# A linear-attention and snake-MLP kernel on one core: all engine orders planned anew, zero matmuls in other places

## The chip, the core and the metric

The kernel runs on one core of one Trainium2 chip. Its engines are TensorE (PE, with its weight loads as PEld), VectorE (DVE), ScalarE (ACT), GpSimd (POOL) and SyncE (SP); SP issues nearly all DMAs. The metric is the device time in microseconds; lower is better.

## The reference

Two layers stand one behind the other. The first is a gated linear attention with a decaying state, the second an MLP whose activation is a snake function:

```python
f = 1.0 / (1.0 + np.exp(-f_logit))                      # batch 4, heads 8, seq 768, head_dim 48
for t in range(S):
    state = f[:, :, t, :, None] * state + np.einsum('bhd,bhe->bhde', k[:, :, t], v[:, :, t])
    y[:, :, t] = np.einsum('bhd,bhde->bhe', q[:, :, t], state)
x = y.transpose(0, 2, 1, 3).reshape(B * S, H * D)       # 3072 tokens x 384
h = x @ w_in                                            # 384 -> 2048
s = np.sin(alpha * h)
out = (h + s * s / (alpha + 1e-09)) @ w_out             # 2048 -> 384
```

## The kernel before, in words

**Work.** The sequence is cut in chunks of 128 tokens, and the attention is done by chunks. The inputs come in 12 units `u` = 0 to 11. A unit has four loads of 384 KB, named here by letter and unit: f5 is the gate logits of unit 5, q5 its queries, k5 its keys, v5 its values. Units 0 to 3 cover two chunks of one batch each, in runs of 384 bytes; units 4 to 11 cover one chunk of two batches each, in runs of 192 bytes (`load`, L247 to L259). A unit holds two pairs, numbered `m` = 2u and 2u + 1. So q5 serves pairs 10 and 11.

**Steps of a unit** (`pre`, L332): ACT takes exp and ln of the gate (L341, L350), PE sums the logs (`cs_`, L359 and L365), ACT makes G and its inverse Gi (L373, L376), and POOL or DVE multiply the keys by Gi and the queries by G (`mul`, L383, tile qk). `values` (L353) casts v to bf16, mostly on POOL.

**Steps of a pair** (`attend_two` for units 0 to 3, `attend` from unit 4): PE transposes keys and queries (`transposed`, L414; called kt and qt with the pair's number here), DVE or ACT copy the result out, PE makes the scores (`a_`, L467 or L549), DVE masks them (L472 or L553), PE makes y from the state (`inter_`, L489 or L558) and from the chunk (`intra_`, L484 or L564) and the new outer products (`kv_`, L497 or L569), and DVE and POOL update the state (L575, L418). From pair 16 on the transposes of keys and queries are DMAs (L586).

**Steps of the MLP.** `x_of` copies y to bf16 (tile yn, L426) and transposes it, for groups 0 to 2 on PE (L430, copied out at L434), for groups 3 to 5 by a DMA from SP (tile xT, L444). A group is 512 tokens, with four y tiles numbered 0 to 3. `first` and `first_half` (L619, L638) make h in PSUM, ACT takes the sine (L604), DVE adds (L607, tile g). `second` (L656) multiplies g by w_out, ACT or DVE copy the result out (tile osb, L662), SP stores it (L666). The weights are loaded in eight pieces into a ring of three buffers (`w_in` L289, `w_out` L311) and folded to bf16 by DVE or ACT (L296, L317, L319).

**What sets the order.** The program first collects all operations (`op`), 956 of them, each with the engines that can run it and a planner's costs. It then issues them in the sequence of the list `ORDER` (`in_order`). An entry x is a packed number: the operation is x modulo 2000, the choice among its engines is x // 2000 % 5, the PSUM bank of the tile that it takes is x // 10000 % 10 (and x // 1000000 for a second tile), and x // 100000 % 10 is a number of zero matmuls that PE runs ahead of it. A zero matmul is 128 x 512 elements of a zeroed tile, written to the bank that the next operation takes (L704); it has no result that is used. The engines run their own queues in this order, each strictly from front to back, and wait for one another by semaphores. The buffers in SBUF come from rings (`SLOTS`), and a load waits until its buffer is free. The costs and the `dma=` figures in the source were the planner's inputs; `in_order` doesn't read them, so only `ORDER` reaches the chip.

Of the kernel before, what the change touches and what calls it, by code (L numbers as in the profile page):

```python
# [17 lines left out]

ORDER = [2, 78, 79, 720081, 82, 6, 140, 141, 400143, 40144, 60000, 4, 84, 3, 86, 90, 83, 10, 2085, 50091, 92,
    2088, 2089, 70095, 96, 5, 1, 202, 7, 145, 94, 2080, 2130105, 93, 14, 2097, 8, 2087, 63, 51, 98, 146, 40099,
    147, 102, 106, 240, 70153, 150, 2151, 130157, 2148, 100, 2149, 203, 4060101, 241, 103, 9, 107, 158, 50062,
    2160, 1030104, 109, 108, 154, 2110, 2152, 205, 159, 2155, 2113, 64, 30111, 65, 2112, 55, 206, 20050, 208,
    156, 207, 30114, 59, 40243, 60164, 2115, 2211, 20244, 100161, 130054, 53, 52, 246, 12, 165, 245, 2142, 162,
    20119, 7060167, 150116, 168, 2210, 120, 56, 117, 40163, 1050166, 57, 2172, 171, 60122, 2175, 121, 169, 170,
    40173, 16, 123, 118, 176, 2177, 2248, 2174, 10125, 2213, 30137, 20134, 40187, 124, 126, 66, 15, 11, 127, 69,
    50178, 58, 138, 139, 135, 188, 70184, 60181, 136, 2068, 179, 61, 10199, 247, 30193, 60, 189, 180, 2249, 212,
    131, 182, 2067, 20190, 40716, 50253, 254, 209, 250, 72, 185, 132, 717, 183, 60128, 2214, 186, 256, 75, 255,
    70215, 216, 13, 50726, 194, 195, 727, 133, 30196, 736, 71, 2070, 129, 737, 738, 739, 200, 201, 191, 18, 218,  # L30
    728, 10706, 729, 2217, 707, 130, 60219, 192, 2073, 2251, 220, 70257, 258, 718, 2074, 17, 77, 2252, 740, 197,
    222, 259, 221, 2260, 719, 720, 721, 2204, 198, 22, 310, 708, 709, 20, 60226, 76, 20223, 730, 311, 227, 741,
    722, 710, 349, 742, 224, 743, 2242, 744, 60313, 40314, 19, 723, 316, 20264, 23, 315, 731, 350, 724, 732,
    733, 24, 40229, 265, 2318, 2322, 2734, 7060225, 2321, 7030228, 2234, 20261, 711, 26, 230, 233, 2237, 231,
    40352, 40353, 735, 262, 317, 60235, 320, 712, 2070267, 232, 354, 21, 359, 236, 268, 30263, 6030266, 25, 355,
    2360, 713, 60323, 70238, 272, 271, 324, 269, 30, 30273, 2714, 2275, 10336, 239, 2274, 70375, 276, 2357, 28,
    325, 270, 376, 40326, 356, 337, 745, 2277, 20286, 420, 2358, 377, 60378, 33, 2338, 40287, 421, 288, 328,
    327, 379, 2312, 40302, 10362, 363, 303, 364, 329, 2361, 60294, 330, 304, 60295, 282, 296, 289, 305, 283,
    297, 20278, 284, 60279, 285, 40298, 280, 40299, 38, 37, 60290, 4351, 281, 20291, 306, 2528, 2319, 60307,
    300, 20766, 767, 292, 301, 30776, 768, 34, 27, 777, 40423, 60424, 778, 293, 308, 426, 309, 769, 60372, 373,  # L40
    70346, 770, 771, 425, 457, 772, 559, 365, 40339, 347, 773, 60333, 70380, 381, 779, 2429, 2428, 780, 340,
    725, 29, 374, 2774, 781, 526, 782, 31, 366, 20341, 458, 40746, 430, 342, 783, 747, 460, 432, 461, 49, 2784,
    382, 431, 343, 70367, 427, 334, 32, 368, 30331, 369, 20433, 527, 434, 748, 50445, 60344, 348, 446, 70385,
    749, 750, 435, 462, 467, 715, 2422, 463, 2447, 345, 335, 20370, 383, 2465, 332, 386, 2371, 2384, 751, 752,
    60436, 2468, 20448, 50450, 2387, 449, 753, 408, 20409, 560, 437, 2754, 20392, 410, 40442, 443, 40393, 394,
    775, 411, 60388, 36, 389, 390, 2466, 40482, 395, 483, 2651, 451, 2452, 396, 60397, 2469, 39, 20400, 401,
    2484, 398, 42, 50438, 439, 391, 60404, 440, 46, 60405, 43, 40412, 413, 453, 399, 785, 464, 402, 406, 444,
    414, 416, 60417, 403, 30796, 20756, 407, 797, 60562, 418, 415, 757, 758, 2459, 40563, 798, 40454, 40, 419,
    564, 799, 50470, 471, 529, 565, 20530, 800, 41, 759, 760, 455, 60485, 472, 40473, 570, 486, 761, 532, 569,
    762, 531, 801, 10786, 755, 2537, 816, 474, 35, 60479, 649, 650, 70487, 488, 763, 817, 764, 2489, 441, 536,  # L50
    802, 40475, 787, 44, 566, 535, 534, 70556, 20491, 818, 788, 582, 476, 549, 803, 492, 804, 4561, 789, 819,
    820, 490, 2477, 478, 790, 20583, 40550, 791, 792, 2571, 456, 624, 493, 625, 793, 821, 480, 2538, 45, 557,
    60585, 822, 584, 2794, 70552, 823, 551, 20589, 2568, 805, 48, 586, 553, 40494, 40495, 558, 533, 2554, 795,
    587, 496, 60518, 824, 506, 590, 60519, 520, 539, 497, 40507, 508, 20502, 20503, 40498, 20499, 521, 2567,
    2626, 60510, 509, 47, 504, 500, 60511, 806, 807, 808, 809, 501, 505, 810, 40652, 40653, 811, 812, 512, 813,
    513, 20627, 40628, 655, 10836, 837, 657, 572, 654, 2656, 838, 588, 60540, 40573, 2814, 839, 826, 827, 828,
    629, 481, 765, 829, 574, 40846, 541, 630, 20514, 515, 2633, 50575, 825, 632, 830, 2659, 576, 658, 555,
    60522, 516, 2634, 40523, 847, 848, 849, 850, 840, 577, 517, 50542, 841, 660, 591, 524, 831, 631, 842, 667,
    20661, 525, 662, 60668, 843, 543, 669, 2544, 851, 852, 832, 50546, 833, 642, 834, 578, 20856, 30579, 580,
    635, 581, 545, 853, 857, 670, 2844, 858, 859, 547, 671, 2854, 60636, 845, 40643, 30663, 637, 860, 2672, 644,  # L60
    861, 862, 548, 855, 863, 2864, 608, 40609, 610, 673, 835, 664, 2665, 60596, 20597, 598, 815, 666, 20645,
    611, 40592, 593, 30638, 639, 604, 594, 599, 646, 20605, 2647, 640, 595, 60600, 20601, 606, 641, 607, 20612,
    40866, 602, 613, 648, 620, 603, 867, 614, 621, 622, 615, 623, 865, 60616, 868, 50896, 897, 898, 899, 900,
    617, 869, 870, 20694, 20695, 901, 618, 876, 619, 696, 877, 878, 902, 903, 871, 60674, 697, 10886, 904, 872,
    879, 880, 20678, 873, 20675, 676, 874, 20679, 40686, 60687, 677, 881, 882, 887, 60690, 883, 888, 691, 680,
    688, 2884, 681, 689, 905, 692, 20682, 906, 683, 693, 907, 40698, 60699, 684, 875, 885, 685, 60702, 20703,
    20936, 937, 908, 938, 909, 939, 940, 910, 30916, 941, 704, 917, 705, 918, 60926, 927, 928, 929, 919, 889,
    700, 701, 942, 943, 911, 912, 913, 2914, 930, 931, 932, 933, 934, 944, 915, 920, 921, 890, 891, 922, 923,
    2924, 945, 925, 892, 893, 935, 70946, 947, 948, 949, 950, 951, 952, 894, 895, 953, 2954, 955]

SLOTS = dict(f=3, k=3, q=3, v=3, lf=2, qk=6, vb=4, gl=6, Gi=2, tr=4, at=3, xT=2, yn=4, s=3, g=18, G=2, osb=4, sum=2,
             wst=3, st0=2, st1=2, st2=2, st3=2)
# [15 lines left out]
def in_order(ops):  # L88
# [5 lines left out]
    held = {n: [(None, -1)] * k for n, k in SLOTS.items()}  # L94
    for nth, x in enumerate(ORDER):
        o = ops[x % 2000]
# [15 lines left out]
def kernel(  # L112
# [19 lines left out]
    B, H, S, D = q.shape  # L132
# [18 lines left out]
    PE, ACT, DVE, POOL, SP = "PE", "ACT", "DVE", "POOL", "SP"  # L151
# [10 lines left out]
    def op(engs, emit, deps=(), takes=(), holds=(), table=None, dma=None, after=0):  # L162
        o = Op(engs, emit, [d for d in deps if d is not None], list(takes), table, dma, after)
        o.uses = set(takes) | set(holds)
        for b in o.uses:
            b.users.append(o)
        ops.append(o)
        return o
# [10 lines left out]
    def at(b):  # L179
        return T[b.ring][b.place]  # L180
# [66 lines left out]
    def load(u, n):  # L247
        b = bufs[n, u] = Buf(n)

        def emit(e):  # L250
            if u < B:
                dst = at(b).rearrange("c (h j) d -> c h (j d)", j=2)
                src = srcs[n][u * H:(u + 1) * H, :2 * C, :].rearrange("h (c j) d -> c h (j d)", j=2)
            else:
                c, bp = divmod(u, NU)
                dst = at(b)
                src = srcs[n][bp * 2 * H:(bp + 1) * 2 * H, c * C:(c + 1) * C, :].rearrange("b c d -> c b d")
            engine[e].dma_start(out=dst, in_=src)  # L258
        b.ready = op({SP: 500}, emit, takes=[b], dma=1240 if u < B else 1800)  # L259

    bufs, made = {}, {}

# [409 lines left out]
    for u in range(NCH * NU):  # L672
        for n in "fkqv":
            load(u, n)
# [61 lines left out]
```

## Time and profile before

| | |
|---|---|
| median of 5 runs | 184.59 us (184.44 to 185.94) |
| span of the profiled execution | 184.5 us |
| device time of the profiled execution | 186.25 us |
| PE busy | 175.1 us, 95% |
| DVE, ACT, POOL busy | 138.3, 126.6, 65.3 us |
| DMA moved | 33.48 MB, 181 GB/s on average |

The profiled execution took 186.25 us, of which 184.5 lie between its first and its last instruction; it is 1.66 us above the median of the runs that were not profiled. Its rows are compared with its own span, and only differences are carried over to the median. PE is shown as busy while a matmul is anywhere in its pipeline, so the durations of single matmuls overlap; the time that one costs is read from start to start.

### The profile page before, as it was taken

What the parts mean: (1) busy time and instruction counts of PE and PEld (TensorE: products, weight loads), DVE (VectorE), ACT (ScalarE), POOL (GpSimd) and SP (SyncE); (2) the same over time, 40 slices, a digit from 0 to 9 for tenths busy, and PEclk for the clock granted to TensorE, in tenths of its full rate; (3) what the DMA queues carried; (4) which work ended last, traced back from release to release, by engine and by line L of the source; (5) the groups of instructions that cost most, each with busy time, mean ns of one, the idle gap of its engine ahead of it and who ended that gap; (6) DMA issues with size and microseconds to landing.
All of it is one profiled execution on the core that took longest, in us unless ns stands there. A gap on an engine that the chain in (4) does not pass through costs nothing.

```text
span 184.5 us, 4401 instructions
## 1 busy us (share of the span) xinstructions
PE 175.1 (95%) x1773; PEld 107.4 (58%) x1773; DVE 138.3 (75%) x185; ACT 126.6 (69%) x171; POOL 65.3 (35%) x107
## 2 busy tenths in 40 slices
PE   6698999899996999999999999999999999999993
PEld 2366678666673546675556764455675555555662
DVE  4679999898885898888697885799785874375511
ACT  2959997789786989899979557895336744164311
POOL 7396215661486202959304783047030000000000
DMA  5999999999999999999999869938733310111014
GB/s 156 322 335 358 320 310 273 317 331 198 192 156 240 197 249 219 213 239 230 224 205 193 182 137 261 179 96 101 151 110 107 62 45 4 43 45 40 0 68 149
DMA packets 103516, 33.48 MB, mean 181 GB/s; under 512 B 96684, under 2 KB 101948, under 8 KB 103496
## 3 DMA queue, kind: packets, MB, share of 16 engines
q1 hardware_dynamic: 103440, 33.17, 76.4%
q8 instruction: 14, 0.23, 0.5%
q14 instruction: 6, 0.05, 0.1%
q10 hardware_dynamic: 56, 0.03, 0.1%
HBM read 25.20 MB, written 4.72 MB: 162 GB/s over the span
## 4 chain that ended last, share of the span: by engine, by line
PE 71%; DMA 17%; SPq 4%; ACT 3%; POOL 1%; DVE 1%; issue 1%; POOLq 0%; ACTq 0%
PE banks L619 28%; PE banks L656 27%; DMA wst<-in_moe_w_out_dram 5%; DMA v<-in_v_dram 4%; DMA q<-in_q_dram 4%; PE banks L359 3%; SPq L258 3%; PE banks L414 3%; DMA xT<-yn 2%; PE banks L549 2%; DMA f<-in_f_logit_dram 2%; PE banks L564 2%; PE banks L558 1%; PE banks L365 1%; PE banks L704 1%; PE banks L569 1%
## 5 line engine op out<-in xcount | busy, mean ns | idle before, releaser
L656 PE MATMUL banks<-w_out_bf,g 128*128 128x384 bf16 (+1 forms) x400 | 72.3, 320 | 0.0
L607 DVE SCALAR_TENSOR_TENSOR g<-s,banks 128x1024 bf16<-128x1024 f32 (+1 forms) x56 | 57.4, 1064 | 15.3 <-ACT s L604 15.2
L604 ACT ACTIVATE s<-banks 128x1024 f32<-128x1024 f32 (+1 forms) x56 | 49.2, 902 | 20.0 <-PE banks L619 19.5
L619 PE MATMUL banks<-xT,w_in_bf 128*128 128x512 bf16 x240 | 56.4, 379 | 0.2 <-DMA xT<-yn 0.2
L656 PEld LDWEIGHTS <-g 128*128 128x128 bf16 x400 | 36.1, 98 | 21.1
L619 PEld LDWEIGHTS <-w_in_bf 128*128 128x128 bf16 x240 | 22.5, 98 | 23.9 <-issue 0.2
L383 POOL TENSOR_TENSOR qk<-q,G 128x384 bf16<-128x384 f32 x18 | 18.7, 1047 | 21.8 <-PE banks L359 8.4
L383 POOL TENSOR_TENSOR qk<-k,Gi 128x384 bf16<-128x384 f32 x20 | 20.4, 1032 | 17.0 <-DMA v<-in_v_dram 9.6
L553 DVE TENSOR_TENSOR at<-banks,mask 128x1024 bf16<-128x1024 f32 x16 | 18.8, 1218 | 4.2 <-PE banks L549 4.0
L662 ACT COPY osb<-banks 128x384 f32<-128x384 f32 (+1 forms) x14 | 6.6, 468 | 15.2 <-PE banks L656 15.2
L353 POOL CAST vb<-v 128x768 bf16<-128x768 f32 x10 | 9.1, 911 | 19.7 <-DMA v<-in_v_dram 19.7
L341 ACT ACTIVATE f<-f 128x768 f32<-128x768 f32 x12 | 10.0, 845 | 5.1 <-DMA f<-in_f_logit_dram 5.1
L414 PE MATMUL banks<-ident,qk 128*128 128x128 bf16 x128 | 10.7, 224 | 2.5 <-POOL qk L383 2.4
L662 DVE COPY osb<-banks 128x384 f32<-128x384 f32 (+1 forms) x11 | 5.8, 536 | 9.6 <-PE banks L656 9.6
L418 POOL TENSOR_TENSOR st<-sum,gl 128x384 bf16<-128x384 f32 x11 | 9.4, 858 | 8.7 <-DVE sum L575 8.7
L426 ACT CAST yn<-banks 128x384 bf16<-128x384 f32 x15 | 7.1, 480 | 7.8 <-PE banks L564 7.5
L702 ACT ACT_TABLE_LOAD x9 | 11.5, 1283 | 0.2
L638 PE MATMUL banks<-xT,w_in_bf 128*128 128x256 bf16 x96 | 11.6, 273 | 0.0
L414 PEld LDWEIGHTS <-qk 128*128 128x128 bf16 x128 | 8.4, 101 | 4.7 <-POOL qk L383 3.3
L376 ACT ACTIVATE Gi<-banks 128x768 f32<-128x768 f32 x12 | 9.8, 813 | 1.4 <-PE banks L365 1.2
L373 ACT ACTIVATE G<-banks 128x776 f32<-128x776 f32 (+1 forms) x12 | 9.8, 820 | 0.6 <-PE banks L365 0.3
L350 ACT ACTIVATE lf<-f 128x768 bf16<-128x768 f32 x12 | 10.0, 846 | 0.2
(93 smaller groups left out, 194.6 us busy)
## 6 DMA issues: line engine op xcount, KB each, us to landing
f<-in_f_logit_dram SPq DMA_DIRECT2D x12, 384.0 KB, 5.3
q<-in_q_dram SPq DMA_DIRECT2D x12, 384.0 KB, 5.0
k<-in_k_dram SPq DMA_DIRECT2D x12, 384.0 KB, 5.8
v<-in_v_dram SPq DMA_DIRECT2D x12, 384.0 KB, 5.4
out_dram<-osb SPq DMA_DIRECT2D x23, 192.0 KB, 2.1
wst<-in_moe_w_in_dram SPq DMA_DIRECT2D x4, 768.0 KB, 6.4
wst<-in_moe_w_out_dram SPq DMA_DIRECT2D x4, 768.0 KB, 7.9
xT<-yn SPq DMA_TRANSPOSE x12, 2.3
```

What stands on the lines that cost most here:

```text
L341: nc.scalar.activation(out=at(fb_), in_=at(fb_), func=Act.Exp, scale=-1.0)
L350: nc.scalar.activation(out=dst, in_=src, func=Act.Ln, bias=1.0)
L383: engine[e].tensor_mul(at(qkb)[:, x, :, :, :D].rearrange("c p r d -> c (p r) d"), heads(at(src), u, i), g[:, i, :H * D].rearrange("c (h d) ...
L414: nc.tensor.transpose(ps(tpb, 1024, BF16)[:, (x * HP + p) * C:(x * HP + p + 1) * C], at(qkb)[:, x, p, :, :].rearrange("c r e -> c (r e)"), ...
L553: nc.vector.tensor_mul(at(atb).rearrange("c r p t -> c (r p) t"), ps(ab, 1024).rearrange("c (x t) -> c x t", t=C), mask.unsqueeze(1).to_br ...
L604: nc.scalar.activation(out=at(sb)[:, :n], in_=ps(hb, n), func=Act.Sin, bias=QUARTER)
L607: nc.vector.scalar_tensor_tensor(take(at(gb)), at(sb)[:, :n].rearrange("p (j t) -> p j t", j=2), -1.0, ps(hb, n).rearrange("p (j t) -> p j ...
L619: nc.tensor.matmul(ps(hb, 2 * TOK)[:, j * TOK:(j + 1) * TOK], w_in_bf[:, kb, f * P:(f + 1) * P], at(xb)[:, :, kb, :], start=(kb == 0), sto ...
L638: nc.tensor.matmul(h[:, j, :], w_in_bf[:, kb, (fb + j) * P:(fb + j + 1) * P], at(xb)[:, ts, kb, :], start=(kb == 0), stop=(kb == KB - 1))
L656: nc.tensor.matmul(ps(ob, n), at(bufs["g", c, fb])[:, j - fb, t * P:(t + 1) * P], w_out_bf[:, j, ms], start=(j == 0), stop=(j == FB - 1))
L662: (nc.scalar.copy if e == ACT else nc.vector.tensor_copy)(at(sbuf)[:, :n], ps(ob, n))
L702: nc.scalar.preload_act_table_set(now)
```

## The change

The list `ORDER` is replaced as a whole. It still names each of the 956 operations once. 51 of them run on another engine, among ACT, DVE and POOL; the number of operations on ACT goes from 156 to 154, on DVE from 166 to 168, and stays at 76 on POOL, 457 on PE and 101 on SP. The planner's figure for a 192-byte load goes from 1800 to 1930 ns.

```diff
-ORDER = [2, 78, 79, 720081, 82, 6, 140, 141, 400143, 40144, 60000, 4, 84, 3, 86, 90, 83, 10, 2085, 50091, 92,
-    2088, 2089, 70095, 96, 5, 1, 202, 7, 145, 94, 2080, 2130105, 93, 14, 2097, 8, 2087, 63, 51, 98, 146, 40099,
...
+ORDER = [2, 78, 79, 700081, 6, 60082, 140, 3, 141, 83, 2088, 84, 4, 10, 202, 203, 89, 240143, 86, 85, 5, 120095,
+    14, 70000, 30091, 1, 96, 97, 92, 2098, 2080, 144, 6070105, 8, 93, 7, 94, 145, 2087, 100099, 90, 146, 20102,
...
-        b.ready = op({SP: 500}, emit, takes=[b], dma=1240 if u < B else 1800)
+        b.ready = op({SP: 500}, emit, takes=[b], dma=1240 if u < B else 1930)
```

The lists are numbers; unpacked, they read as follows at the places that the prediction speaks of.

| place | before | changed |
|---|---|---|
| zero matmuls (16 in both) | 7 ahead of the sums of unit 0, 4 ahead of those of unit 1, then 1 each ahead of kv 0, kt 3, a score of unit 1, a w_in spread, the first `first_half` | 7 ahead of the sums of unit 0, 2 ahead of those of unit 1, then 1 each ahead of kt 1, a score of unit 0, kt 2, a w_in spread, and 3 ahead of kt 3 |
| PE, first steps | sums 0, sums 1, kt 0, qt 0, kt 1, qt 1, kv 0 | sums 0, first half of sums 1, kt 1, kt 0, qt 1, qt 0, second half of sums 1, kv 0 |
| SP, loads ahead of q5 | f0 f1 q0 k0 f2 v0 k1 f3 q1, four weights with v1 among them, q2 q3, wout0, k3 k2, wout1 wout2 wout3, v2 f4 v3 f5 q4 k4 k5 | the same 29 in another order: f0 f1 k0 q0 f2 v0 f3 q1 k1, the four, wout0, k3 q3 q2 k2, wout1, v2, wout2 wout3, f4 v3 f5 k4 q4 k5 |
| SP, behind q5 | f6, store, v4 v5 f7 q6, store, v7 f9 v8 f8 k6 | f6 k6 f7 v4 v5 f8, store, v6 q6 k8 f9 k7 |
| PE about q5 | kt 9, kt 11, one y transpose, **qt 11**, score 8, qt 9, `first` of group 1 | kt 9, three y transposes and the state's carry, kt 11, qt 9, score 8, **qt 11**, `first` of group 1 |
| POOL about q5 | q8, q9, k8, k9, k11, q11, q10, k10 multiplied | k9, k8, q8, q9, k11, q11, k10, q10 multiplied |
| POOL thereafter | v4, v8 cast, q12, a state, k13 | v4, v6, v5 cast, q12, a state, k13 |
| `kv_` of pair 13 on PE | behind `first` of group 2, entry 226 of PE's 457 | ahead of it, entry 173 |
| y of pair 14 to `first` of group 3 | entries 254 and 273 of PE | entries 254 and 273 of PE |
| `second`, first product with w_out pieces of wout1 | in row tile 3 of group 0, entry 65 of PE | in row tile 1, entry 60 |
| end of PE's queue | half of the last row tile alone | the other half of it, mixed with tiles 0, 1 and 2 of group 5 |

## The prediction

> **What bounds the kernel now.** I read the page first: the span, the busy times, the slices.
>
> ```profile
> span 184.5 us, 4401 instructions
> PE 175.1 (95%) x1773; PEld 107.4 (58%) x1773; DVE 138.3 (75%) x185; ACT 126.6 (69%) x171; POOL 65.3 (35%) x107
> ...
> PE   6698999899996999999999999999999999999993
> ...
> DMA  5999999999999999999999869938733310111014
> ```
>
> PE is the bound: 95% busy, and after slice 12 no slice but the last is under 9. A plan can't shorten PE's work, and the changed list has the same 457 PE operations and 16 zero matmuls. It can only move waits. So I asked next what PE waited for.
>
> ```profile
> PE banks L414 <- POOL qk L383: 2.4, 2, 1.8
> PE banks L359 <- ACT lf L350: 2.0, 1, 2.0
> ...
> PE banks L619 <- DMA xT<-yn: 0.2, 1, 0.2
> ```
>
> The 2.0 us for lf are the first gate load with its exp and ln; f0 and f1 stay in front, so this wait stays. The longest that a plan can touch is the 1.8 us for POOL. The chain of waits says where it comes from, the timeline what PE did.
>
> ```profile
> 49.42 7.00 DMA q<-in_q_dram
> ...
> 56.56 1.00 POOL qk L383
> 57.56 0.05 issue
> 57.61 0.40 PE banks L414 x4
> ```
>
> ```profile
> 55.48 0.33 PE L430 MATMUL banks<-ident,yn 128*128 128x128 bf16 x3
> ...
> 57.61 0.40 PE L414 MATMUL banks<-ident,qk 128*128 128x128 bf16 x4 [1.79 <-POOL qk L383]
> ```
>
> q5 is issued at 49.42 and lands at 56.42. POOL multiplies it until 57.56, and PE, through with its last y transpose at 55.7 (0.22 us after 55.48, from start to start), begins qt 11 at 57.61. From there to 181.6, where PE's last matmul ends, the rows show one more wait, at 111.3. Why was q5 late? The DMA view of 52.5 to 57 us (a digit is 0.11 us) shows near idleness just before it lands:
>
> ```profile
> DMA  9999999999953111000100000467799999999999
> ...
> q8 instruction: 1, 0.02, 1.6%
> ```
>
> The trace's completions of q5 tell the rest: fifteen of sixteen parts by 54.68, the last at 56.42. In between lies one 16 KB instruction fetch (53.05, 1.15 us). It comes when PE has executed some 1324 instructions, and holds one DMA engine. The other engines soon idle, as SP's next issue waits for the slow one.
>
> **The change, part by part.**
>
> *The wait for q5.* The same 29 loads stand ahead of q5 in both lists, and the DMA slices ahead of it are at 9, so their order moves its landing little: I keep 56.42. POOL takes q11's product first among those that need q5 in both lists, so qt 11 can start at 57.6 in both. What differs is what PE does before it waits. The changed list has qt 9 and the scores of pair 8 ahead of qt 11, which the old list had behind it; otherwise the two sets are the same. From start to start qt 9 costs 0.22 us (four transposes at 56 ns) and the scores 0.25. They move into a wait of 1.8: **-0.47 us**.
>
> *Everything ahead of that wait.* The start is different almost everywhere: k0 before q0, k1 third behind f3 and q1, two zeros fewer ahead of unit 1, kt 1 ahead of the second half of unit 1's sums. By the rows the first mask comes some 0.7 us earlier (kh 1 done near 9.6, all four transposes by 12.1, the scores near 13.6 where they began at 13.88), while unit 1's key product waits for k1, third instead of first of its three loads: near 14.1 instead of 12.56. Later SP has v2 ahead of wout2, which spares it the wait for a free weight buffer, and the pairs 4 to 7 are transposed later, when their products are long made; two PE waits go (0.29 and 0.75 us from start to start at 34.6 and 36.4). Against that the first product with wout1 comes earlier, at 27.4 us of PE work instead of 28.6. wout1 landed at 36.85 and ACT folded until 38.05, and the old order had done 27.4 us of work at 38.3; so whatever is gained before, PE stands at about the same place at 38. I cost all of it at **0**: it is hidden by what is left of the wait for q5, 1.8 - 0.47 = 1.3 us. If the start loses more than 1.3 us, the rest counts in full; a gain counts nothing.
>
> *Zero matmuls.* They fill time on PE until its clock is up.
>
> ```profile
> 8.09 1.87 PE L704 MATMUL banks<-zeros 128*128 128x512 bf16 x4
> ...
> 11.78 1.42 PE L414 MATMUL banks<-ident,qk 128*128 128x128 bf16 x16
> ```
>
> The four zeros from 8.09 on start about 0.42 us apart; late in the start-up one costs 0.22. In the second row the first four transposes take 0.41 us and the third four 0.22: the speed doubles near 12.6. The Trainium skill ("TensorE: Matmul & The Clock Gate", Part 1) says that PE reaches full speed after about 3.4 us of sustained work, counted in a free-running window. By the rule alone seven zeros over 3.2 us and the work from 6.39 on would have done it by 9.8, and two zeros fewer would cost nothing. The row gives 6.2 us from 6.39. If thinner work in the new start let one more window of 3.4 us pass at half speed, PE would be some 1.7 us late. I go with the row, speed at 12.6, since my walk leaves PE no gap there: **0**, at most +0.4 (1.7 less the cover of 1.3).
>
> *Group 3's xT.* At 111.3 PE waited 0.33 us (start to start) for the last xT. Its y was done near 105.9, SP issued the transpose at 107.16 and it landed at 111.19, fifteen parts by 109.46: again an instruction fetch, at 109.02. Between the start of that y and the first matmul of group 3 stand 5.18 us of PE work in the old list and 4.98 in the new; fetches follow PE's instruction count, so it should come at the same place. **+0.20 us**.
>
> *Group 2's start* is tighter. Two x copies move from ACT to DVE (0.59 us each in the row of L434), the second ready near 82.9 where PE arrives near 82.7: **+0.15**, between 0 and 0.5.
>
> *Moved to other engines, moved loads, wait order on SP.* DVE keeps its 166 to 168 operations, POOL its 76, and PE hides both while no operation comes before its input. I found one place where a new order asks more: POOL casts v6 and v5 ahead of q12, a state and k13, and `kv_` of pair 13 now follows on PE near 77.3 us (19.4 us of work behind qt 11, times 1.017, the pace of the old trace there), not at 97.8. v6 is the eighth transfer behind q5: seven loads at 1.83 us (steps of 1.81 to 1.87 between landings at 67 to 74 us) and a store at 0.58 make 69.8; both casts end by 71.5. G of unit 6 comes from ACT near 73.5; then q12 1.0, a state 0.86, two small ones 0.4, k13 1.0: 76.8. Margin 0.5 us: **0**, with a tail.
>
> *The planner's 1930* reaches no instruction: **0**. *The end*: again a half-width tile last (0.32 us of ACT and a store); the store of a full tile just ahead was there before too: **0**, up to +0.3.
>
> Sum: -0.47 + 0.20 + 0.15 = -0.12 us against the profiled span of 184.5. That execution stands at 186.25 with what lies outside its span, 1.66 above the median. Some of its waits may belong to profiling, so I carry over the difference alone: 184.59 - 0.12, about **184.5 us**.
>
> **Rivals.**
>
> *A new wait (slower).* The margin of 0.5 us at pair 13 is smaller than what one fetch does to a load: q5's last part came 1.74 us after the others, f5's 1.48, k2's 2.4. If v6, q6 or the sums of unit 6 are late so that q12 starts after 74.0 instead of 73.5, each further microsecond is PE's, for POOL is a queue and k12 stands behind (kt 12 is needed near 79). There is cover nowhere: the wait for q5 lies before. One such lag costs 1.74 - 0.5 = 1.2 us, two or a stretched POOL product (1.51 instead of 1.0 at 9.16) 2 to 2.5. With the -0.12: 185.7 to 186.9. For it: the need moved forward 20 us. Against: the old list had such margins too, and shows no wait between 58 and 110.
>
> *q5 lands in time (faster).* If the fetch misses q5, it lands at 54.7, and k11's and q11's products end by 55.9; PE arrives at 56.2 (55.7 + 0.47) instead of 57.6 with the same work behind it plus 0.47: -1.9 us, 182.7. Against: the instruction count at this place is the same to within two, so the fetch should come at 53 again. It could be had in part, if the order before it puts PE off by a microsecond.
>
> *The x of group 3 and of group 2 come free (a little faster).* Without the two additions and without the old 0.33: -0.47 - 0.33 = -0.8, 183.8; still within what counts as no change.
>
> **How the numbers follow.** About 0.5% (0.92 us) is what a measurement of this kernel can tell from no change: under 183.67 is faster, over 185.51 slower. Forecast: 0.38. New wait behind q5, or a start that loses more than its cover: 0.37, of which 0.03 stays below 185.51. q5 in time, or other waits gone: 0.25, of which 0.03 gets no further than 183.8. That makes faster 0.22, same 0.38 + 0.03 + 0.03 = 0.44, slower 0.34. The forecast's own range is 183.7 to 185.3 (the unknown ends of the parts: -0.8 to +0.7). Eight times in ten: from 182.7, the early q5, to 186.9, two lags.
>
> **What would show it.** Right: PE busy 175 us again; a wait of 1.2 to 1.5 us at qt 11 with the last part of q5 near 56.4; `first` of group 1 some 0.5 us earlier than 58.50; group 3's first matmul waiting 0.3 to 0.6 us for xT. Wrong: waits of PE for POOL or DVE between 58 and 110 (pair 13, or x of group 2); an arrival at qt 11 after 57.6; q5 complete by 55; PE at half speed after 13.5.

## The result, and the profile after

The changed kernel takes 183.83 us (median of 37 runs, 182.81 to 185.28) where the kernel before takes 184.64 (median of 72, 182.97 to 187.74). The ratio is 0.9966, with a 95% interval of 0.9949 to 0.9983: about 0.6 us less, a real gain, and less than the 0.5% that the prediction set as its bound of no change. (All ratios count only the fast runs of a kernel, those within 1.5% of its fastest, so this one is smaller than the distance of the two medians.) A second comparison, with one of the groups of experiments below, gave 0.9942 (0.9913 to 0.997).

The profiled execution of before that the prediction read (186.25 us) was one of its late ones. So a second execution of the same kernel (184.45 us) is used beside it here.

The page of the changed kernel, its span, busy times and slices:

```profile
span 181.1 us, 4393 instructions
...
PE 173.9 (96%) x1772; PEld 107.6 (59%) x1773; DVE 137.4 (76%) x187; ACT 124.9 (69%) x170; POOL 65.6 (36%) x107
...
PE   7698999999998999999999999999999999999993
...
DMA  5999999998999999999998879888722400120204
```

PE is the bound as before, 96% busy. All of PE's waits in this execution (total, times, longest):

```profile
PE banks L360 <- ACT lf L351: 1.7, 1, 1.7
PE banks L705 <- DVE zeros L189: 1.3, 1, 1.3
PE banks L415 <- POOL qk L384: 0.8, 2, 0.6
PE banks L485 <- DVE at L473: 0.3, 1, 0.3
```

The two long ones lie in the start-up. Of the wait for POOL at qt 11, 0.6 us is left where the first profile had 1.8; the wait of group 3 for xT is gone. The chain of waits still goes through q5, which lands at 47.60 + 6.34 = 53.94 us:

```profile
47.60 6.34 DMA q<-in_q_dram
...
54.07 1.01 POOL qk L384
55.09 0.05 issue
55.13 0.40 PE banks L415 x4
```

In the first execution of before q5 had landed at 56.42. That is the largest difference between the two first traces, 2.5 us, and a reader who stopped here would call the earlier load the gain. The experiments below speak against it.

### The profile page after: what moved, and what is told of

Same layout as the page of the kernel before. It is cut to its first block, busy times and chain, and to the rows that moved or that the text cites. A ratio compares the mean times of both kernels' runs of the same rounds, so it can differ in the third digit from the quotient of the medians.

```text
span 181.1 us, 4393 instructions
## 1 busy us (share of the span) xinstructions
PE 173.9 (96%) x1772; PEld 107.6 (59%) x1773; DVE 137.4 (76%) x187; ACT 124.9 (69%) x170; POOL 65.6 (36%) x107
## 4 chain that ended last, share of the span: by engine, by line
PE 69%; DMA 15%; POOL 7%; SPq 3%; ACT 2%; DVE 1%; issue 1%; POOLq 0%; ACTq 0%
PE banks L657 29%; PE banks L620 29%; DMA q<-in_q_dram 7%; POOL qk L384 7%; DMA k<-in_k_dram 6%; PE banks L550 2%; SPq L259 2%; PE banks L415 2%; DMA f<-in_f_logit_dram 2%; PE banks L565 2%; PE banks L559 2%; PE banks L570 1%; PE banks L360 1%; DVE w_in_bf L297 1%; ACT lf L351 1%; ACT f L342 1%
## 5 line engine op out<-in xcount | busy, mean ns | idle before, releaser
L657 PE MATMUL banks<-w_out_bf,g 128*128 128x384 bf16 (+1 forms) x400 | 71.5, 320 | 0.0
L620 PEld LDWEIGHTS <-w_in_bf 128*128 128x128 bf16 x240 | 22.4, 98 | 23.1
L384 POOL TENSOR_TENSOR qk<-q,G 128x384 bf16<-128x384 f32 x19 | 20.1, 1058 | 23.2 <-PE banks L657 10.5
L354 POOL CAST vb<-v 128x768 bf16<-128x768 f32 x9 | 7.5, 843 | 23.2 <-DMA v<-in_v_dram 23.1
L427 ACT CAST yn<-banks 128x384 bf16<-128x384 f32 x17 | 7.9, 478 | 7.0 <-PE banks L565 6.6
L419 POOL TENSOR_TENSOR st<-sum,gl 128x384 bf16<-128x384 f32 x11 | 10.0, 911 | 6.7 <-DVE sum L576 4.9
L663 DVE COPY osb<-banks 128x384 f32<-128x384 f32 x11 | 6.1, 554 | 6.0 <-PE banks L657 5.2
L639 PEld LDWEIGHTS <-w_in_bf 128*128 128x128 bf16 x96 | 9.1, 98 | 1.3
```

The lines of the kernel that those rows point to most:

```text
L384: engine[e].tensor_mul(at(qkb)[:, x, :, :, :D].rearrange("c p r d -> c (p r) d"), heads(at(src), u, i), g[:, i, :H * D].rearrange("c (h d) ...
L620: nc.tensor.matmul(ps(hb, 2 * TOK)[:, j * TOK:(j + 1) * TOK], w_in_bf[:, kb, f * P:(f + 1) * P], at(xb)[:, :, kb, :], start=(kb == 0), sto ...
L639: nc.tensor.matmul(h[:, j, :], w_in_bf[:, kb, (fb + j) * P:(fb + j + 1) * P], at(xb)[:, ts, kb, :], start=(kb == 0), stop=(kb == KB - 1))
L657: nc.tensor.matmul(ps(ob, n), at(bufs["g", c, fb])[:, j - fb, t * P:(t + 1) * P], w_out_bf[:, j, ms], start=(j == 0), stop=(j == FB - 1))
L663: (nc.scalar.copy if e == ACT else nc.vector.tensor_copy)(at(sbuf)[:, :n], ps(ob, n))
```

## The experiments

All kernels of one group ran on one chip, each compared with the kernel before there. The diffs are written with the operations' names, since the lists hold only numbers. All of them do the whole computation; only orders and zero matmuls differ.

### The kernel before again

```diff
 (no edit)
```

> The kernel before, unchanged: a second profiled execution, and the comparison of a kernel with itself. If the instruction fetch follows PE's instruction count, as the prediction assumed, the last part of q5 lands again 1.5 to 2 us behind the fifteenth (before: 56.42 behind 54.68), PE waits again 1.5 to 2 us at qt 11, and group 3's first matmul waits again some 0.3 us for xT. If the place of the fetch against the loads is a matter of the single execution, the lag of q5 is under 1 us or the wait at qt 11 differs by over 0.5 us. The time ratio should be 1.000 within 0.002 by either theory.

Ratio 0.9999 (0.997 to 1.0027); the profiled execution took 184.45 us. q5 landed at 54.76, fifteen of its parts by 53.35, in place of 56.42 and 54.68. PE's waits in this execution, without the two in its first 7 us, again total, times, longest:

```profile
PE banks L413 <- POOL qk L382: 1.1, 1, 1.1
PE banks L483 <- DVE at L471: 0.3, 1, 0.3
PE banks L466 <- DVE tr L459: 0.2, 1, 0.2
```

The lag of the last part came back (1.41 us), with its instruction fetch (at 51.26, PE instruction 1287). But the landing itself moved by 1.66 us and the wait at qt 11 by 0.7, with the same list. Group 3 did not wait for xT. So a single landing of q5 can't be put down to an order; what can be compared between kernels is the time from it onward. In this execution PE begins qt 11 (first row), group 1 (second row, 2.08 us after q5's landing) and the scores of pair 11 (third row) as follows:

```profile
55.95 0.40 PE L413 MATMUL banks<-ident,qk 128*128 128x128 bf16 x4 [1.13 <-POOL qk L382]
...
56.84 0.81 PE L618 MATMUL banks<-xT,w_in_bf 128*128 128x512 bf16 x3
57.58 0.40 PE L548 MATMUL banks<-tr 64*128 64x128 bf16 x8
```

### The two operations alone

```diff
 PE: ... kt 11, y transpose,
-    qt 11, scores 8, qt 9, first of group 1 ...
+    qt 9, scores 8, qt 11, first of group 1 ...
```

> The kernel before with one edit: qt 9 and the scores of pair 8 ahead of qt 11 on PE, as in the changed order; nothing else moves. Theory 1 (the prediction's first term): they fill 0.47 us of the wait for q5, so 0.47 us less, ratio 0.9975, and the wait at qt 11 is shorter by 0.47 than in the second execution of before. Theory 2 (the changed kernel gains because q5 itself lands earlier, through other orders of the loads and of the start): most of the gain isn't here, the ratio is 0.9975 at most and q5 lands where it does in before. Theory 3 (the gain is in the tail behind qt 11): ratio 1.000 if the two products are only shifted and PE meets another wait in their stead.

Ratio 0.9994 (0.9969 to 1.0019). The gain of 0.47 us that the prediction booked was not seen; the interval still allows it. The trace says where it may have gone. Group 1's first matmul came 1.46 us after q5's landing where both executions of before show 2.08: the two operations do fill the wait, and are worth 0.62. Then two new waits follow, 0.30 us at the scores of pair 11 and 0.28 at y of pair 8 (start to start, less the work between). The timeline of PE in this execution, and the chain that ends at the second one:

```profile
55.15 0.40 PE L413 MATMUL banks<-ident,qk 128*128 128x128 bf16 x4
55.38 0.83 PE L618 MATMUL banks<-xT,w_in_bf 128*128 128x512 bf16 x3
56.33 0.40 PE L548 MATMUL banks<-tr 64*128 64x128 bf16 x8
```

```profile
53.60 5.02 DMA v<-in_v_dram
58.62 0.05 issue
58.68 0.83 POOL vb L352
59.51 0.04 issue
59.55 0.36 PE banks L563 x8
```

The scores (L548) need DVE's copy of the transposes of pair 11, which is there 1.17 us after qt 11 begins (next experiment). In the second execution of before these scores began 1.63 us after qt 11 (55.95 to 57.58), with scores 8, qt 9 and a group of `first` in between. With the two moved away only qt 11 itself and the group of `first` are left, 0.22 + 0.65 = 0.87 us, and 0.30 of waiting fills it up to 1.17. And y of pair 8 (L563) needs v4, the next load but one behind q5. So the stall moved 1 and 4 us on. (All matmuls of this execution ran 2 to 3% longer, 327 ns against 320 in the row of `second`; its later stages are not compared.)

### More work into the wait, in the old order

```diff
 PE: ... kt 11, y transpose,
-    qt 11, scores 8, qt 9, first of group 1 (fb 4), scores 11 ...
+    qt 9, scores 8, first of group 1 (fb 4), qt 11, scores 11 ...
```

> The kernel before with qt 9, the scores of pair 8 and the first matmul group of group 1 (0.65 us) ahead of qt 11: 1.1 us of work moved into a wait of 0.9 to 2.0 us. If q5's landing sets the end, the distance from it to group 1's first matmul falls from 2.08 to about 0.8 us and the time by 0.9 to 1.3: ratio 0.993 to 0.995, no worse than the changed kernel. If the waits only move on behind qt 11 (kt 10, a 11, the masks of group 1), ratio 0.998 to 1.000.

Ratio 0.999 (0.9961 to 1.0019). The wait at qt 11 is gone altogether, group 1 begins 0.58 us after q5's landing in place of 2.08, and no gain is seen. PE's waits between 53 and 84 us:

```profile
PE banks L548 <- DVE tr L582: 0.8, 1, 0.8
PE banks L563 <- POOL vb L352: 0.6, 1, 0.6
```

and the first of them in the timeline, behind qt 11:

```profile
56.38 0.39 PE L413 MATMUL banks<-ident,qk 128*128 128x128 bf16 x4
57.55 0.40 PE L548 MATMUL banks<-tr 64*128 64x128 bf16 x8 [0.79 <-DVE tr L582]
```

57.55 - 56.38 = 1.17 us is the shortest way from qt 11 through DVE's copy to the scores. Group 1 began 1.5 us sooner after the landing, and waits of 0.95 and 0.74 us (start to start) followed at the scores of pair 11 and at y of pair 8. So in both executions in which work was moved into the wait without anything moved behind it, the stall came back. By their intervals the two edits may still be worth up to 0.6 and 0.7 us.

### The changed kernel again

```diff
 (no edit to the changed kernel)
```

> The changed kernel itself on this chip, with a second profiled execution. By the first comparison the ratio is 0.9966, about 0.65 us less. In its first execution PE's clock doubled late (near 12.3 us), and still q5 landed at 53.94 and the run took 182.92. If the changed order makes q5 land early whatever the clock does, q5 lands again by 54.2 and the wait at qt 11 is again under 1.2 us. If it was the luck of one execution, q5 lands after 54.5 here.

Ratio 0.9942 (0.9913 to 0.997). q5 landed at 55.38: the 53.94 of the first trace was luck. PE around qt 11:

```profile
55.61 0.40 PE L550 MATMUL banks<-tr 64*128 64x128 bf16 x8
56.57 0.40 PE L415 MATMUL banks<-ident,qk 128*128 128x128 bf16 x4 [0.56 <-POOL qk L384]
56.80 1.46 PE L620 MATMUL banks<-xT,w_in_bf 128*128 128x512 bf16 x6
58.09 0.39 PE L415 MATMUL banks<-ident,qk 128*128 128x128 bf16 x4
58.32 0.81 PE L620 MATMUL banks<-xT,w_in_bf 128*128 128x512 bf16 x3
58.97 0.39 PE L415 MATMUL banks<-ident,qk 128*128 128x128 bf16 x4
59.28 0.40 PE L550 MATMUL banks<-tr 64*128 64x128 bf16 x8
```

Read it against the experiment before: behind qt 11 (56.57) stand two groups of `first`, kt 10, a third group and qt 10, and only then the scores of pair 11 at 59.28. That is 2.71 us, where DVE's copy asks for 1.17 at the least. y of pair 8 follows at 72.65, 12 us later than in the old order (60.48), long after v4. So in the changed order both of the next stalls have cover, and neither shows in its traces. No run moves this cover alone into the old order, so that it is what keeps the 0.66 us is read from the traces and not tested by itself. A new small wait appears further back, y of pair 17 waiting in group 3 for a bank that DVE still copies out:

```profile
111.09 0.33 PE L559 MATMUL banks<-st,tr 128*128 128x96 bf16 x4 [0.44 <-DVE osb L663]
```

### Old start, changed rest

```diff
-ORDER = [the changed order]
+ORDER = [entries 1 to 306 of the order before, then all others as in the changed order]
```

> The first 306 entries of the order before (start-up, and all loads to q5 and f7 in the old sequence, with the old zero matmuls), then all other operations in the changed order. Theory 1 (the order of the loads ahead of q5 moves nothing; the gain is the two products in the wait and the freed xT of group 3): the whole gain remains, ratio 0.996 to 0.997 as for the changed kernel, and q5 lands within 0.5 us of where it lands in before. Theory 2 (the loads come earlier because SP doesn't wait for weight buffers): the gain falls by what q5 is late, at least half of it, ratio 0.998 to 1.000. Theory 3 (the tail): ratio as for the changed kernel.

Ratio 0.9926 (0.9896 to 0.9957), median 183.19 us: the gain is all there with the old start, the old loads to q5 and the old place of the zero matmuls. So it comes from what stands behind entry 306: PE around q5 and all after it. q5 landed at 53.93. The ratio came out lower than the changed kernel's, so it was timed again:

> The order with the first 306 old entries and the changed rest, timed a second time: its first comparison gave 0.9926 with an interval of 0.9896 to 0.9957, lower than the changed kernel's 0.9966 and 0.9942. If the old start is better than the new one, it stays under 0.994. If the difference was chance, since q5's landing differs by 2.5 us between executions of one kernel, it comes out at 0.995 to 0.997 like the changed kernel.

Ratio 0.9883 (0.9848 to 0.9918), median 183.44 where the kernel before took 185.87. q5 landed at 55.04. Both ratios lie under both of the changed kernel's, but the two kernels were not run in one group, so the distance between them (0.4 and 0.6%, from ratios of different groups) is not measured directly. One pair in this last group does compare the two starts, with qt 11 moved in both (last experiment): 183.96 us with the changed start (6 runs) and 184.21 with the old one (12 runs). There the old start is not the better one, so whether it is better at all stays open. q5 landed at 53.94, 55.38, 56.62 and 55.21 in the four executions with the changed start and at 53.8 to 56.4 in the nine with the old one, too few and too far apart to show a difference.

### Old start-up only

```diff
-ORDER = [the changed order]
+ORDER = [entries 1 to 100 of the order before, then all others as in the changed order]
```

> The first 100 entries of the order before (first twelve or so microseconds: loads f0 f1 q0 k0 f2 v0, the sums of units 0 and 1 with 7 and 4 zero matmuls), then the changed order. It tells whether the start-up is part of the gain. Theory 1 (the start-up is hidden by the wait for q5): ratio as for the changed kernel, 0.996 to 0.997. Theory 2 (the start-up brings loads forward): less of it, 0.998 to 1.000, with k2 and q5 landing about 1 us later than in the changed kernel.

Ratio 0.9978 (0.9957 to 0.9999). q5 landed at 53.10, the earliest of all, and helped nothing: PE reached qt 11 only at 55.84 and did not wait there. It had lost 1.60 us (start to start) at 21 us, in front of the first group, where it waited for DVE's mask:

```profile
PE banks L637 <- DVE at L471: 1.4, 1, 1.4
```

So a load that comes earlier pays no further than PE's own arrival.

### Old order to behind q5, changed tail

```diff
-ORDER = [the order before]
+ORDER = [entries 1 to 420 of the order before, then all others as in the changed order]
```

> The first 420 entries of the order before (all up to some 40 PE operations behind the wait for q5, PE's first 169 operations), then the changed order: the tail alone, with groups 2 and 3, their x, pair 13's kv early and the loads behind q6 in the changed sequence. From the first matmul of group 1 to PE's last the executions took 123.1 and 122.95 (before), 122.5 (changed), 122.99 and 123.26 (changed tail behind an old head). Theory 1 (the tail gives 0.1 to 0.5, the rest comes from ahead of and at q5): ratio 0.9975 to 1.000. Theory 3 (the tail gives most): ratio 0.994 to 0.996, as the order with the first 306 old entries had. Theory 4 (the early kv of pair 13 costs, as the prediction's slower rival had it): over 1.002 with a wait of PE near 77 us.

Ratio 1.0213 (1.016 to 1.0265): 4 us slower. This joint makes the prediction's slower rival come true. `kv_` of pair 13 stands early on PE, as in the changed order, but the loads stand in the old order, with v6 landing at 76.88 where the changed kernel has it at 67.23. Four views of this execution follow: POOL's timeline, PE's waits from 56 to 90 us, PE's timeline behind the longer wait, and a table by stretches (after the length of a stretch: PE, PEld, DVE, ACT, POOL busy, the granted clock, the DMA share, GB/s).

```profile
77.00 0.82 POOL L352 CAST vb<-v 128x768 bf16<-128x768 f32 x1 [3.42 <-DMA v<-in_v_dram]
77.79 0.83 POOL L417 TENSOR_TENSOR st<-sum,gl 128x384 bf16<-128x384 f32 x1
78.58 0.20 POOL L378 TENSOR_TENSOR gl<-G,bd 128x8 f32<-128x8 f32 x1
78.74 0.99 POOL L382 TENSOR_TENSOR qk<-k,Gi 128x384 bf16<-128x384 f32 x1
```

```profile
PE banks L568 <- POOL qk L382: 2.1, 1, 2.1
PE banks L557 <- ACT yn L425: 0.5, 1, 0.5
```

```profile
81.30 1.06 PE L413 MATMUL banks<-ident,qk 128*128 128x128 bf16 x8
```

```profile
80.00:82.00 2.00, 2.00 (x32) 1.66 (x29) 0.92 (x2) 0.48 (x1) 2.00 (x3) 0.59 1.27 226
82.00:84.00 2.00, 2.00 (x24) 1.60 (x21) 0.69 (x1) 0.77 (x2) 0.24 (x1) 0.55 1.24 253
84.00:86.00 2.00, 1.87 (x17) 1.09 (x15) 1.68 (x4) 1.44 (x4) 1.17 (x2) 1.00 1.20 236
```

POOL is a queue: its cast waits 3.42 us for v6, the product of k13 stands behind it, and `kv_` behind that. The wait of 2.06 us then costs more than itself, since PE's clock drops: the granted clock (third number from the right) is 0.59 and 0.55 from 80 to 84 us. From start to start transposes take 107 ns there, 56 before and after. The two waits cost 2.8 us (start to start). The work from 80.37 to 83.84, 3.47 us here, takes 1.91 us in the changed kernel (75.49 to 77.40): half speed costs some 1.6 us.

In the changed kernel itself the product of k13 ends at 73.94 and `kv_` begins at 74.91: a margin of 1.0 us (75.37 and 76.35 in its second execution). The joint moves a need without the load that feeds it; the change moves both.

### More zero matmuls at the start

```diff
-        for _ in range(idle):
+        for _ in range(11 if idle == 7 else idle):
```

> The kernel before with 11 zero matmuls instead of 7 ahead of the first sums, so that PE works without a gap from 1.26 us to about 6, where the 7 end at 4.2. In the six profiled executions so far PE's speed doubled before 6.2 in two, near 10 in one, and at 12.3 to 12.5 in three, with the same first seven zeros. Theory A (the phase of the clock moves PE by a microsecond in the start, this moves the instruction fetches against the loads, and the loads to q5 land up to 2 us apart): with the speed doubled by 8.1 in each execution, q5 lands near 54 and the median falls by 0.5 to 1.0 us, ratio 0.995 to 0.997, with a narrower spread. Theory B (the start is hidden by the waits for wout1 and q5, as the prediction had it): ratio 0.999 to 1.001, the spread stays. Loss by the sums waiting for a last zero: at most 0.2 us.

> The changed kernel with the same 11 instead of 7 zero matmuls ahead of the first sums. Theory A: 0.2 to 0.6 us under the changed kernel, less than the edit brings to the kernel before, since the changed order had q5 early even with a late clock; ratio to the kernel before 0.993 to 0.9955. Theory B: as the changed kernel, ratio 0.9966 within 0.001.

On the kernel before: 0.9963 (0.993 to 0.9997); on the changed one: 0.9951 (0.9917 to 0.9986), no better than the 0.9942 that it has without. The edit does what it says: four zeros and the gates of unit 1 run at the doubled speed. First the second execution of before, then this one:

```profile
8.06 1.87 PE L703 MATMUL banks<-zeros 128*128 128x512 bf16 x4
```

```profile
7.46 1.02 PE L703 MATMUL banks<-zeros 128*128 128x512 bf16 x4
...
10.67 1.09 PE L413 MATMUL banks<-ident,qk 128*128 128x128 bf16 x16 [1.00 <-DVE qk L382]
```

But PE then waits 1.00 us for the first product, and q5 landed at 53.80 in the one kernel and at 56.62, later than in any other trace, in the other. An early clock did not bring q5 early in both: theory A falls as the cause of the landings. For the kernel before, an interval that ends at 0.9997 leaves a gain of anything up to 1.3 us; what it would come from is open. With 11 zeros in both, the two orders lie only 0.12% apart (184.92 and 184.64 us in one group), with intervals that overlap: this pair does not show the gain of the changed order by itself.

### qt 11 behind two groups of `first`

```diff
 PE: ... qt 9, scores 8,
-    qt 11, first of group 1 (fb 4, fb 6), kt 10 ...
+    first of group 1 (fb 4, fb 6), qt 11, kt 10 ...
```

> The changed kernel with one edit: qt 11 stands behind the first two matmul groups of `first` of group 1 (fb 4 and fb 6, 1.29 us of PE work that needs nothing of unit 5), no longer ahead of them. In the executions so far the time from q5's landing to group 1's first matmul was 2.08 us in the old order and 1.42 in the changed one, whatever q5's landing was, so q5 set the end. If so, the wait at qt 11 (0.71 to 1.05 in the changed order) goes, group 1's first matmul starts within 0.8 us of q5's landing, and the time falls by 0.4 to 0.8 under the changed kernel: ratio to the kernel before 0.991 to 0.994. Rival: the loads behind q5 or the copies of x set the pace too, and PE waits the same time a little later (at kt 10, qt 10 or group 2): ratio as for the changed kernel, 0.994 to 0.9966.

> The old first 306 entries, then the changed order, with qt 11 behind the same two matmul groups. By the first theory 0.3 to 0.6 us under the same kernel without the move (wait there 0.62): ratio to the kernel before near 0.990 if the 0.9926 of its first comparison holds, 0.991 to 0.993 if that was high by chance. By the rival no lower than that kernel.

On the changed kernel 0.989 (0.9848 to 0.9932), six runs; on the kernel with the old first 306 entries 0.9917 (0.9882 to 0.9952), where that kernel without the move had 0.9883 in the same group. The wait at qt 11 is gone in both traces. PE then waits 0.29 and 0.39 us at `first` itself (start to start), and y of pair 17 waits 0.95 and 0.44. From q5's landing to PE's last matmul they take 124.70 and 124.30 us, no less than without the move (next section). So the traces show no gain from the move, and the runs don't resolve one.

## Why the prediction was right, and where it was not

The forecast was 184.5 us with no measurable change; measured were 183.83 and a ratio of 0.9966, inside the range and within the 0.5%. The traces give this balance. PE's last matmul ends so long after q5's landing, in the executions with undisturbed matmuls:

| kernel | q5 lands | to group 1's first matmul | from there to PE's last end | sum |
|---|---|---|---|---|
| before, first execution | 56.42 | 2.08 | 123.10 | 125.18 |
| before, second execution | 54.76 | 2.08 | 122.95 | 125.03 |
| before with 11 zeros | 53.80 | 2.08 | 123.98 | 126.06 |
| before, more work in the wait | 55.16 | 0.58 | 125.13 | 125.71 |
| changed, first | 53.94 | 1.43 | 122.71 | 124.14 |
| changed, second | 55.38 | 1.42 | 123.30 | 124.72 |
| changed with 11 zeros | 56.62 | 1.42 | 122.71 | 124.13 |
| old 306 entries, then changed | 53.93 | 1.42 | 122.99 | 124.41 |
| the same, second | 55.04 | 1.42 | 122.69 | 124.11 |

The sum is 125.0 to 126.1 with the old order behind q5, and 124.1 to 124.7 with the changed one. (The order with the old start-up only is not in the table: PE itself came late there, 2.97 us passed from the landing to group 1, and the sum was 126.23.) The landing itself differs by up to 2.7 us among executions that start in the same order, more than the whole gain. For the runs without a trace it can't be read, but a spread of that size is what their times show (182.8 to 185.3 and 183 to 187.7).

Point by point:

- **The wait for q5 (-0.47).** The place and the sign were right. The term was mis-sized a little (2.08 - 1.42 = 0.66: the two operations cost 0.22 and 0.25 of work and some 0.2 of stepping between them). What failed is its reason. The step "the changed list has qt 9 and the scores of pair 8 ahead of qt 11, which the old list had behind it; otherwise the two sets are the same" looked only ahead of qt 11. The two operations were also the cover between qt 11 and the scores of pair 11. Moved alone they showed no gain. In the changed list kt 10, qt 10 and two more groups of `first` stand in that gap and y of pair 8 stands far back, and so, by the traces, the term holds. The prediction counted neither of these: that its largest term came out was luck.
- **q5's landing ("I keep 56.42").** Wrong as a figure: 53.1 to 56.6 in the executions. It cost the sum nothing, as both kernels have it alike. The reason that was given, a fetch that follows PE's instruction count, holds for the lag of the last part (0.8 to 1.7 us in all executions but one; in all 14 traces a fetch falls into q5's transfer, at PE instruction 1269 to 1324, so the rival in which it misses q5 never came) but not for the landing. What moves the stream of loads ahead of it stays open; no run takes it apart.
- **All ahead of that wait (0), zeros (0).** Hidden to within what these runs show; the runs don't say which start is the better one. The clock's doubling near 12.6 was one of several places: in executions with the same first seven zeros it came before 6.3 (two), near 10 (two) or between 12 and 12.8 (seven), and in one it was there by 6.65 and gone again from 9.5 to past 13. The Trainium skill ("TensorE: Matmul & The Clock Gate", Part 1) says that the window is free-running and that the place differs from run to run by about half a microsecond; here it differed by more than six. I had taken one row for a rule.
- **Group 3's xT (+0.20).** Did not come. The old wait was itself in the execution: 0.33 us in the first, none in the second. In its place the changed order has a wait for a bank at y of pair 17, nothing in the first execution and 0.61 us (start to start) in the second; six of the nine executions with the changed order at this place have it, with 0.30 to 0.95 us. The prediction had no term for it.
- **Group 2's start (+0.15).** Did not come: in both changed executions group 2's first matmul begins 0.15 us after the last matmul ahead of it (80.50 and 81.93), without a wait.
- **Pair 13 (0, margin 0.5).** Right: no wait, margin 1.0. The rival's price was too low: in the experiment whose changed tail stood behind the old order, a wait of 2 us there came with 4 us more in all, for the clock dropped.
- **The end (0).** Right: device time less PE's last end is 4.84 and 4.71 us in the changed executions, 4.65 and 4.66 in those of before.

Signed, the sum forecast -0.12 us. It kept the one true gain and added two losses that were not there: without these it is -0.47, with the size as measured -0.66, where the first comparison gives 0.34% of 184.64 = 0.63 us. The second (0.58%) allows some tenths more in the tail, whose spread (122.7 to 123.3 against 122.95 to 123.98) neither shows nor excludes it.

## What to carry to other kernels

An operation that is moved ahead of a wait leaves a gap behind it. Before you book it as gained, count the work that then stands between the late operation and its first dependent, and compare it with the copy in between (here 1.17 us). When a load's landing scatters by more than the effect, measure from the landing, not from the start, and take a second trace of the kernel before ahead of any story about the first. A need that is moved forward must take its load with it.

## What the hardware showed that I had not expected

- A single wait of PE of 2.06 us, with 0.45 us of waiting shortly before, was followed by a halved clock for about 3.45 us (80.35 to 83.8): 2.8 us of waiting and some 1.6 us of half speed. The Trainium skill ("TensorE: Matmul & The Clock Gate", Part 1) lets the clock fall after at least one idle window of about 3.4 us; here less idle time was enough.
- With 11 zeros ahead the speed doubled near 5.05 us in both kernels, some 3.8 us after the first zero at 1.26. With 7 zeros, which end at 4.2, it had doubled by 6.3 in two executions, and in most others not before 12.
- The same list of loads brought the 30th of them at times 1.66 us apart in two executions of one program, and 2.6 us apart over all executions with that list.
